# GEGLU feed-forward on one core: program order on every queue but TensorE's, smaller W loads at the half change, and a tail bank by bank

## The chip, the cores and the metric

The kernel runs on one core of a Trainium2 chip. The metric is device time in microseconds for one execution. The core has five engines with a queue each: TensorE (PE in the profile; its weight loads are PEld), VectorE (DVE), ScalarE (ACT), GpSimdE (POOL) and SyncE (SP), which here does nothing but issue DMA transfers. Matmuls write to PSUM, which this kernel divides into 8 banks of 128 x 512 float32.

## What is computed

```python
B, S, D, F = 1, 2048, 1024, 3584      # all bfloat16
def reference(x, w_gate, w_up, w_down):
    return (_gelu(x @ w_gate) * (x @ w_up)) @ w_down     # gelu, tanh form
```

## The kernel before

**Halves.** The 2048 tokens are worked in two halves of 1024 (loop over `h`). For each half the kernel first makes `hT` = gelu(gate) * up, 28 blocks of 128 rows of F by 1024 tokens, and then multiplies it by w_down (`down`). The names `t1`, `bank`, `wd_sb` and so on in the profile are the tiles' names in the code.

**Startup (h = 0 only).** Nine warm matmuls on constants (L164) run while the first data arrives. The first 512 tokens of x come in by plain loads and are transposed on TensorE (L229, evacuated at L209 and L211); the second 512 come in by one transposing DMA (L144). `first_units` then works on three blocks of F at once (NSU = 3, six banks: banks 2 to 7), each with a gate sum and an up sum. For each block ScalarE takes the gelu of the gate sum (`gelu`, L186) and VectorE multiplies it by the up sum (`mult`, L190). After that come five plain units (`unit`, 16 matmuls each at L176, two banks each in rotation): block 3 for the first 512 tokens in banks 0 and 1, then blocks 0 to 3 for the second 512 tokens in banks 2 and 3, 4 and 5, 6 and 7, 0 and 1. A bank can be written again only when its gelu or multiply has read it.

**Pairs.** The remaining blocks are worked two at a time (`pair_quads`) by a Strassen-Winograd scheme: 7 products where the plain form has 8, for gate and for up (j = 0 and 1). It needs four sums and one copy of x blocks (`t1` to `t4`, `b22`, made by `t_sums` at L276 to L280 on VectorE, ScalarE and GpSimdE) once for each half, and four sums and one copy of W blocks (`s1` to `s4` on GpSimdE at L301 to L309, `a22` on ScalarE at L311) for each pair. The sums for the next pair are made during the present one, each in a buffer that TensorE has just read. The half h = 0 has 12 pairs, h = 1 has 14.

**W loads.** w_gate and w_up come in chunks of 512 columns (`new_chunk`, `load_w`), 1 MB each, with two buffers for each matrix; `load_w` for a whole chunk is two transfers of 1 MB.

**Down.** `down` goes over two groups of 512 tokens, each in 14 steps `kk`. A step takes one tile of w_down (`wd_sb`, 512 KB, three buffers) and does 16 matmuls (L423), two in each of the 8 banks; the banks are finished in the last step of the group. ScalarE and VectorE then cast them to bfloat16 (L435, L459), and SyncE stores whole rows. In the very last bank the work is split in two half banks (L444 on VectorE, L451 on ScalarE), each with a store of its own.

**Half change.** During `down` of h = 0 a list `fillers` brings in what h = 1 begins with: each step takes one entry. In the kernel before the entries are one empty, one for all of W chunk 0 (2 MB), 16 transposing loads of x, the sums of W, one for all of W chunk 1 (2 MB), one empty, and the sums of x.

**Order.** A scheduler puts the instructions on each engine's queue. It goes by program order, but may draw one ahead that it takes to be ready earlier. The helper `sp` chains the transfers on SyncE in program order with dependences that order the queue and add no semaphore. `after` does the same for the x sums alone: it puts them behind the last transposition copies, not behind the gelus.

Of the kernel before, what the change touches and what calls it, by code (L numbers as in the profile page):

```python
# [31 lines left out]
def kernel(  # L32
# [67 lines left out]
    last_sp = [None]  # L100

    def sp(inst):

        if last_sp[0] is not None:
            tc.add_manual_dep(
                inst.ins, last_sp[0].ins.name, SCHED_DEP, reason="SP queue order"
            )
        last_sp[0] = inst
        return inst

    def after(inst, other):
        tc.add_manual_dep(inst.ins, other.ins.name, SCHED_DEP, reason="engine order")
        return inst
# [60 lines left out]

    def mm_gu(ps, w_sb, fi, tb, kd):
        return nc.tensor.matmul(  # L176
            ps[:],
            lhsT=w_sb[:, kd, fi * P : (fi + 1) * P],
            rhs=xT[:, kd, tb * TB : (tb + 1) * TB],
            start=(kd == 0),  # L180
            stop=(kd == KD - 1),
        )

    def gelu(ps):
        g_sb = g_pool.tile([P, TB], F32, name="g_sb")
        nc.scalar.activation(out=g_sb[:], in_=ps[:], func=ACT.Gelu_apprx_tanh)  # L186
        return g_sb

    def mult(hT, g_sb, ps, fc, tb):
        nc.vector.tensor_tensor(  # L190
            out=hT[:, fc, tb * TB : (tb + 1) * TB],
            in0=g_sb[:],
            in1=ps[:],
            op=ALU.mult,
        )
# [9 lines left out]
    last_evac = {}  # L205

    def evac(dst, src):
        if evac_ctr[0] % 2 == 0:
            last_evac["dve"] = nc.vector.tensor_copy(out=dst, in_=src)  # L209
        else:  # L210
            last_evac["act"] = nc.scalar.copy(out=dst, in_=src)  # L211
        evac_ctr[0] += 1
# [29 lines left out]
    def first_units(hT):  # L242
        groups = [warm, transpose_x_piece(0)]
        held = [(banks[2 + 2 * u], banks[3 + 2 * u]) for u in range(NSU)]
        bank_ctr[0] = 0
        for kd in range(KD):
            if kd == KPQ - 1:
                bank_ctr[0] = 0
                groups.append(transpose_x_piece(1))
            g = []  # L250
            for j, w_sb in enumerate(chunks[(0, 0)]):
                g += [mm_gu(held[u][j], w_sb, u, 0, kd) for u in range(NSU)]
            groups.append(g)
        for ga, gb in zip(groups[:-1], groups[1:]):
            tc.add_manual_dep(
                gb[0].ins, ga[-1].ins.name, SCHED_DEP, reason="startup PE order"
            )
        for u in range(NSU):
            mult(hT, gelu(held[u][0]), held[u][1], u, 0)
        bank_ctr[0] = 0  # L260


    tsum = {}

    def half(j):
        return slice(j * KH, (j + 1) * KH)

    def t_sums(eng4):
        def b(j, l):
            return xT[:, half(j), l * TB : (l + 1) * TB]  # L270

        for name in ("t1", "t2", "t3", "t4", "b22"):
            tsum[name] = t_pool.tile([P, KH, TB], F32R, name=name)
        sub = ALU.subtract
        tt = nc.vector.tensor_tensor
        first = after(tt(out=tsum["t1"][:], in0=b(0, 1), in1=b(0, 0), op=sub), last_evac["dve"])  # L276
        tt(out=tsum["t2"][:], in0=b(1, 1), in1=tsum["t1"][:].bitcast(F32), op=sub)
        after(nc.scalar.copy(out=tsum["b22"][:], in_=b(1, 1)), last_evac["act"])
        after(tt(out=tsum["t3"][:], in0=b(1, 1), in1=b(0, 1), op=sub), first)
        eng4.tensor_tensor(  # L280
            out=tsum["t4"][:], in0=b(1, 0), in1=tsum["t2"][:].bitcast(F32), op=sub
        )
# [8 lines left out]
    def s_sum(h, pair, j, name):  # L291
# [7 lines left out]
        tt = nc.gpsimd.tensor_tensor  # L299
        if name == "s1":  # L300
            tt(out=t[:], in0=a(1, 0), in1=a(1, 1), op=ALU.add)  # L301
        elif name == "s2":
            s1 = ssum[(h, pair, j, "s1")][:].bitcast(F32)
            tt(out=t[:], in0=s1, in1=a(0, 0), op=ALU.subtract)
        elif name == "s3":
            tt(out=t[:], in0=a(0, 0), in1=a(1, 0), op=ALU.subtract)  # L306
        elif name == "s4":
            s2 = ssum[(h, pair, j, "s2")][:].bitcast(F32)
            tt(out=t[:], in0=a(0, 1), in1=s2, op=ALU.subtract)  # L309
        else:  # L310
            nc.scalar.copy(out=t[:], in_=a(1, 1))  # L311
# [4 lines left out]
    def pair_quads(hT, h, pair, nxt):  # L316
# [20 lines left out]

        b11 = xT[:, half(0), 0:TB]
# [3 lines left out]
        for j in range(2):  # L342
            mm(PB[j], j, block(key, j, 0, 0), b11, True)
            nc.scalar.copy(out=banks[QB[j]][:], in_=banks[PB[j]][:])  # L344
        for j in range(2):
            mm(VB[j], j, s(j, "s1"), tsum["t1"], True)
            m5[j] = m_pool.tile([P, TB], F32, name=f"m5_{j}")
            nc.scalar.copy(out=m5[j][:], in_=banks[VB[j]][:])  # L348
            prep(j, "s1")
        for j in range(2):  # L350
            mm(QB[j], j, s(j, "s2"), tsum["t2"], False)
            nc.scalar.copy(out=banks[RB[j]][:], in_=banks[QB[j]][:])  # L352
            nc.vector.tensor_tensor(  # L353
                out=banks[QB[j]][:], in0=banks[QB[j]][:], in1=m5[j][:], op=ALU.add
            )
# [7 lines left out]
        for j in range(2):  # L363
            mm(RB[j], j, s(j, "s3"), tsum["t3"], False)
            nc.vector.tensor_tensor(  # L365
                out=banks[VB[j]][:], in0=banks[RB[j]][:], in1=m5[j][:], op=ALU.add
            )
# [31 lines left out]
    def down(hT, h, fillers):  # L399
        for grp in range(SH // TB):  # L400
            last_grp = h == NH - 1 and grp == SH // TB - 1
            o_sb = {}
            for kk in range(NKK):
                n = (h * (SH // TB) + grp) * NKK + kk
                while len(wd_tiles) < n + 3:
                    if n + 3 > NH * (SH // TB) * NKK:
                        break
                    if h == 0 and grp == 1 and len(wd_tiles) >= 2 * NKK:
# [4 lines left out]
                wd_sb = wd_tiles[n]  # L413
                for b in range(8):
# [3 lines left out]
                    split = last_grp and kk == NKK - 1 and b == 7  # L418
                    for cc, cw in (
                        [(c0, DN // 2), (c0 + DN // 2, DN // 2)] if split else [(c0, DN)]  # L420
                    ):
                        for c in range(WDT):
                            nc.tensor.matmul(  # L423
                                banks[b][:, cc - c0 : cc - c0 + cw],
                                lhsT=hT[:, kk * WDT + c, ts * P : (ts + 1) * P],
                                rhs=wd_sb[:, c, cc : cc + cw],
                                start=(kk == 0 and c == 0),
                                stop=(kk == NKK - 1 and c == WDT - 1),
                                skip_group_check=True,
                            )  # L430
                    if kk < NKK - 1:
                        continue
                    if dn == 0:
                        o_sb[b // 2] = o_pool.tile([P, D], BF16, name="o_sb")
                        nc.scalar.copy(  # L435
                            out=o_sb[b // 2][:, 0:DN], in_=banks[b][:]
                        )
                        if last_grp and b == 6:
                            sp(nc.sync.dma_start(
                                out=out2[r0 : r0 + P, 0:DN], in_=o_sb[3][:, 0:DN]  # L440
                            ))
                    elif split:
                        hh = DN // 2
                        nc.vector.tensor_copy(  # L444
                            out=o_sb[3][:, DN : DN + hh], in_=banks[b][:, 0:hh]
                        )
                        sp(nc.sync.dma_start(
                            out=out2[r0 : r0 + P, DN : DN + hh],
                            in_=o_sb[3][:, DN : DN + hh],
                        ))  # L450
                        nc.scalar.copy(  # L451
                            out=o_sb[3][:, DN + hh : D], in_=banks[b][:, hh:DN]
                        )
                        nc.scalar.dma_start(
                            out=out2[r0 : r0 + P, DN + hh : D],
                            in_=o_sb[3][:, DN + hh : D],
                        )
                    else:
                        nc.vector.tensor_copy(  # L459
                            out=o_sb[b // 2][:, DN:D], in_=banks[b][:]  # L460
                        )
                        sp(nc.sync.dma_start(
                            out=out2[r0 : r0 + P, :], in_=o_sb[b // 2][:]
                        ))


    for h in range(NH):
        hT = hT_pool.tile([P, KF, SH], BF16, name="hT")
        first_pair = 0
        if h == 0:  # L470
            first_units(hT)
            for fi in range(NSU, FPG):
                unit(hT, (0, 0), fi, 0)
            unit(hT, (0, 0), 0, 1)
            t_sums(nc.gpsimd)
# [3 lines left out]
            for name in S_NAMES:  # L479
                for j in range(2):  # L480
                    s_sum(0, first_pair, j, name)
        for pair in range(first_pair, NPAIR):
# [5 lines left out]
            if pair == NPAIR - 1:  # L488
                for _ in range(2):
# [3 lines left out]
        if h + 1 < NH:  # L493
# [3 lines left out]
            def w_fill(nh=nh):  # L497
                new_chunk((nh, 0))
                load_w((nh, 0), 0, KD, nc.sync)

            def w_fill1(nh=nh):
                new_chunk((nh, 1))
                load_w((nh, 1), 0, KD, nc.sync)
# [6 lines left out]
            fillers = [lambda: None, w_fill]  # L510
# [5 lines left out]
            fillers += [s_fill, w_fill1, lambda: None, lambda: t_sums(nc.gpsimd)]  # L516
# [31 lines left out]
```

## Time and profile before

| what | us |
|---|---|
| device time, median of 3 runs | 567.64 (567.29 to 569.09) |
| span of the profiled execution | 567.4 |
| startup, to the first matmul of the first pair | 40.6 |
| 12 pairs of h = 0 | 151.3 |
| down of h = 0, with the half change | 98.3 |
| 14 pairs of h = 1 | 176.5 |
| down of h = 1 | 96.8 |
| from the last matmul to the end | 3.9 |

The stages are read from TensorE's timeline, from the first matmul of one to the first of the next. TensorE is the engine with the most work, so each stage is best read as TensorE's working time plus the time in which it stands or runs slowly. In the rows of a timeline the bracket at the end gives the idle time of that engine ahead of the instruction and what ended it. An instruction's start is when it runs; the time that it stood in its queue behind others does not show in its own row, only as idle time of its engine with the name of the first one's releaser.

### The profile page before, as it was taken

The numbers are of one execution on the slowest core, as the hardware profiler recorded it, in microseconds if no ns is written. First come the engines' busy times: TensorE is split into PE (matmuls) and PEld (weight loads), VectorE is DVE, ScalarE is ACT, GpSimd is POOL, SyncE is SP. The second block draws the span as 40 slices with busy tenths as digits, with TensorE's granted clock in tenths as the row PEclk, the third lists the DMA queues.
The fourth block names the chain that finished last, engine by engine and source line by source line (L and its number), as shares of the span: only waits on it lengthen the run. The fifth ranks groups of instructions, "written<-read, shape, count | busy, mean of one in ns | idle before, by whom it ended". The sixth has DMA issues, their size and how long they took to land.

```text
span 567.4 us, 6748 instructions
## 1 busy us (share of the span) xinstructions
PE 557.3 (98%) x2523; PEld 335.6 (59%) x2523; DVE 175.2 (31%) x241; ACT 200.8 (35%) x343; POOL 248.3 (44%) x216
## 2 busy tenths in 40 slices
PE   8799999999999999999999999999999999999997
PEld 4347767777677544444457776776777764444443
DVE  0613344444433300123034444334444440001001
ACT  2325555555555200101045555555555540001001
POOL 0456777777666060004037776677777700000000
PEclk9899999999999999999999999999999999999999
DMA  9513404133400197698421331404070003446443
GB/s 274 171 47 102 148 2 148 38 111 113 147 2 0 40 309 198 193 260 281 165 76 27 123 106 43 148 1 148 2 258 3 0 1 118 160 160 231 149 148 111
DMA packets 60960, 67.54 MB, mean 119 GB/s; under 512 B 14592, under 2 KB 44672, under 8 KB 60928
## 3 DMA queue, kind: packets, MB, share of 16 engines
q1 hardware_dynamic: 60240, 66.53, 37.3%
q10 hardware_dynamic: 688, 0.59, 0.3%
q8 instruction: 20, 0.33, 0.2%
q14 instruction: 12, 0.10, 0.1%
HBM read 59.77 MB, written 4.19 MB: 113 GB/s over the span
## 4 chain that ended last, share of the span: by engine, by line
PE 92%; DMA 5%; SPq 1%; ACT 0%; issue 0%; ACTq 0%; DVE 0%; DVEq 0%
PE bank L322 58%; PE bank L423 32%; DMA wu_sb<-in_w_up_dram 3%; PE bank L176 3%; DMA wd_sb<-in_w_down_dram 3%; SPq L144 1%; ACT g_sb L186 0%; SPq L127 0%; ACTq L127 0%; DVE o_sb L444 0%; ACT o_sb L451 0%; DVEq L444 0%; ACT a L311 0%; ACTq L186 0%
## 5 line engine op out<-in xcount | busy, mean ns | idle before, releaser
L423 PE MATMUL bank<-wd_sb,hT 128*128 128x512 bf16 x898 | 194.1, 379 | 1.2 <-DMA wd_sb<-in_w_down_dram 1.2
L322 PE MATMUL bank<-t,s 128*128 128x512 f32 x624 | 161.0, 406 | 0.0
L423 PEld LDWEIGHTS <-hT 128*128 128x128 bf16 x898 | 87.7, 98 | 107.3 <-issue 2.3
L322 PEld LDWEIGHTS bank<-t,s 128*128 128x128 f32 x624 | 117.4, 188 | 29.0
L190 DVE TENSOR_TENSOR hT<-g_sb,bank 128x512 bf16<-128x512 f32 x112 | 76.8, 688 | 73.2 <-ACT g_sb L186 33.5
L186 ACT ACTIVATE g_sb<-bank 128x512 f32<-128x512 f32 x112 | 66.5, 597 | 83.9 <-DVE bank L365 49.9
L301 POOL TENSOR_TENSOR s<-wg_sb 128x512 fp32r<-128x512 bf16 x26 | 31.6, 1217 | 136.6 <-PE bank L322 93.9
L353 DVE TENSOR_TENSOR bank<-bank,m 128x512 f32<-128x512 f32 x52 | 36.4, 700 | 114.0 <-ACT bank L352 114.0
L435 ACT CAST o_sb<-bank 128x512 bf16<-128x512 f32 x16 | 9.4, 586 | 155.7 <-PE bank L423 155.7
L459 DVE CAST o_sb<-bank 128x512 bf16<-128x512 f32 x15 | 10.4, 692 | 164.7 <-PE bank L423 137.9
L322 PE MATMUL bank<-xT,wg_sb 128*128 128x512 bf16 x208 | 53.9, 382 | 0.0
L322 PE MATMUL bank<-xT,wu_sb 128*128 128x512 bf16 x208 | 53.4, 379 | 0.0
L322 PE MATMUL bank<-b,s 128*128 128x512 f32 x208 | 51.4, 389 | 0.0
L322 PE MATMUL bank<-t,a 128*128 128x512 f32 x208 | 51.3, 389 | 0.0
L322 PEld LDWEIGHTS bank<-b,s 128*128 128x128 f32 x208 | 39.0, 188 | 8.2
L322 PEld LDWEIGHTS bank<-t,a 128*128 128x128 f32 x208 | 39.0, 188 | 8.1
L306 POOL TENSOR_TENSOR s<-wg_sb 128x512 fp32r<-128x512 bf16 x26 | 30.3, 1167 | 20.9 <-PE bank L322 20.9
L365 DVE TENSOR_TENSOR bank<-bank,m 128x512 f32<-128x512 f32 x52 | 36.4, 700 | 9.9 <-PE bank L322 9.9
L348 ACT COPY m<-bank 128x512 f32<-128x512 f32 x52 | 30.6, 588 | 17.7 <-PE bank L322 17.7
L352 ACT COPY bank<-bank 128x512 f32<-128x512 f32 x52 | 29.6, 570 | 17.0 <-PE bank L322 17.0
L322 PEld LDWEIGHTS <-wu_sb 128*128 128x128 bf16 x208 | 20.3, 98 | 24.7 <-issue 0.3
L344 ACT COPY bank<-bank 128x512 f32<-128x512 f32 x52 | 29.6, 570 | 14.3 <-PE bank L322 14.3
(33 smaller groups left out, 320.6 us busy)
## 6 DMA issues: line engine op xcount, KB each, us to landing
wd_sb<-in_w_down_dram SPq DMA_DIRECT2D x56, 512.0 KB, 3.6
wg_sb<-in_w_gate_dram SPq DMA_DIRECT2D x13, 1024.0 KB, 5.4
wu_sb<-in_w_up_dram SPq DMA_DIRECT2D x13, 1024.0 KB, 7.5
out_dram<-o_sb SPq DMA_DIRECT2D x15, 256.0 KB, 2.2
xs<-in_x_dram SPq DMA_DIRECT2D x2, 512.0 KB, 5.8
wg_sb<-in_w_gate_dram SPq DMA_DIRECT2D x3, 256.0 KB, 6.8
wu_sb<-in_w_up_dram SPq DMA_DIRECT2D x3, 256.0 KB, 7.0
xT<-in_x_dram SPq DMA_TRANSPOSE x17, 4.2
```

The lines of the kernel that those rows point to most:

```text
L176: return nc.tensor.matmul(ps[:], lhsT=w_sb[:, kd, fi * P : (fi + 1) * P], rhs=xT[:, kd, tb * TB : (tb + 1) * TB], start=(kd == 0), stop=(k ...
L186: nc.scalar.activation(out=g_sb[:], in_=ps[:], func=ACT.Gelu_apprx_tanh)
L190: nc.vector.tensor_tensor(out=hT[:, fc, tb * TB : (tb + 1) * TB], in0=g_sb[:], in1=ps[:], op=ALU.mult,)
L301: tt(out=t[:], in0=a(1, 0), in1=a(1, 1), op=ALU.add)
L306: tt(out=t[:], in0=a(0, 0), in1=a(1, 0), op=ALU.subtract)
L322: nc.tensor.matmul(banks[bank][:], lhsT=lhs[:, c, :], rhs=rhs[:, c, :], start=start and c == 0, stop=c == KH - 1, skip_group_check=True,)
L344: nc.scalar.copy(out=banks[QB[j]][:], in_=banks[PB[j]][:])
L348: nc.scalar.copy(out=m5[j][:], in_=banks[VB[j]][:])
L352: nc.scalar.copy(out=banks[RB[j]][:], in_=banks[QB[j]][:])
L353: nc.vector.tensor_tensor(out=banks[QB[j]][:], in0=banks[QB[j]][:], in1=m5[j][:], op=ALU.add)
L365: nc.vector.tensor_tensor(out=banks[VB[j]][:], in0=banks[RB[j]][:], in1=m5[j][:], op=ALU.add)
L423: nc.tensor.matmul(banks[b][:, cc - c0 : cc - c0 + cw], lhsT=hT[:, kk * WDT + c, ts * P : (ts + 1) * P], rhs=wd_sb[:, c, cc : cc + cw], st ...
```

## The change

It has four parts.

1. **Queues in program order.** A helper `on` chains each instruction on ScalarE, VectorE and GpSimdE to the last one on the same engine, as `sp` did for SyncE. The dependences order the queue and add no semaphore. TensorE's order is left to the scheduler.
2. **The x sums are placed among the first gelus.** `t_sums` becomes `t_sum(name)`, called one sum at a time: t1 ahead of the gelus of the three held blocks, t2 behind their multiplies, b22 and t3 behind unit 3, then the sums of W for the first pair behind unit (0, 1), and t4 behind these.
3. **Smaller W loads at the half change.** Each W chunk comes in four pieces of two transfers of 256 KB, one piece a step. Two pieces of chunk 0 stand between the two sets of 8 transposing loads of x, two behind them; chunk 1 comes last. Three tiles of w_down are asked for ahead of the half's last pairs, where it was two.
4. **Last two steps bank by bank.** In the last group, steps 12 and 13 are merged: for each bank the two matmuls of step 12 and the two of step 13, so that the banks finish one after the other. The last bank is no longer split. In the last group VectorE casts the even banks and ScalarE the odd ones, and the last store is issued from ScalarE.

The core of the diff:

```diff
+    last_on = {}
+    def on(engine, inst):
+        if engine in last_on:
+            tc.add_manual_dep(
+                inst.ins, last_on[engine].ins.name, SCHED_DEP, reason="engine order"
+            )
+        last_on[engine] = inst
+        return inst
...
-    def after(inst, other):
-        tc.add_manual_dep(inst.ins, other.ins.name, SCHED_DEP, reason="engine order")
-        return inst
+    def act(inst):
+        return on("act", inst)
...
+    def t_sum(name):
...
+        if name == "t1":
+            dve(tt(out=t[:], in0=b(0, 1), in1=b(0, 0), op=sub))
...
+        elif name == "t4":
+            t2 = tsum["t2"][:].bitcast(F32)
+            pool(nc.gpsimd.tensor_tensor(out=t[:], in0=b(1, 0), in1=t2, op=sub))
+        else:
+            act(nc.scalar.copy(out=t[:], in_=b(1, 1)))
...
-        nc.scalar.activation(out=g_sb[:], in_=ps[:], func=ACT.Gelu_apprx_tanh)
+        act(nc.scalar.activation(out=g_sb[:], in_=ps[:], func=ACT.Gelu_apprx_tanh))
...
+        t_sum("t1")
         for u in range(NSU):
             mult(hT, gelu(held[u][0]), held[u][1], u, 0)
...
+            steps = [[(kk, b) for b in range(8)] for kk in range(NKK)]
+            if last_grp:
+                steps[-2:] = [[(kk, b) for b in range(8) for kk in (NKK - 2, NKK - 1)]]
...
+                    if dn == (1 if last_grp else 0):
+                        act(nc.scalar.copy(out=dst, in_=banks[b][:]))
+                    else:
+                        dve(nc.vector.tensor_copy(out=dst, in_=banks[b][:]))
+                    if last_grp and b // 2 == 3:
+                        st = (nc.sync if dn == 0 else nc.scalar).dma_start(
+                            out=out2[r0 : r0 + P, c0 : c0 + DN], in_=dst
+                        )
...
             first_units(hT)
+            t_sum("t2")
             for fi in range(NSU, FPG):
                 unit(hT, (0, 0), fi, 0)
+            t_sum("b22")
+            t_sum("t3")
             unit(hT, (0, 0), 0, 1)
-            t_sums(nc.gpsimd)
+            for name in S_NAMES:
+                for j in range(2):
+                    s_sum(0, PPG, j, name)
+            t_sum("t4")
             for fi in range(1, FPG):
                 unit(hT, (0, 0), fi, 1)
...
-            if pair == NPAIR - 1:
-                for _ in range(2):
+            if pair == NPAIR - 2:
+                for _ in range(3):
                     load_wd(len(wd_tiles))
...
+            def w_fill(key, k0):
+                if k0 == 0:
+                    new_chunk(key)
+                load_w(key, k0, k0 + WKP, nc.sync)
...
-            fillers = [lambda: None, w_fill]
+            fillers = [lambda: None]
             for tb in range(NTB):
                 for kd in range(KD):
                     fillers.append(
                         lambda tb=tb, kd=kd: load_xT(xT, nh, tb, kd, kd + 1)
                     )
-            fillers += [s_fill, w_fill1, lambda: None, lambda: t_sums(nc.gpsimd)]
+            fillers = fillers[:9] + w_fills[0][:2] + fillers[9:] + w_fills[0][2:]
+            fillers += [s_fill] + w_fills[1] + [t_fill]
```

More of the change, by code (lines that the diff above doesn't have):

```diff
@@ L98, in next_bank, with dve, pool @@
         return b
-    last_sp = [None]
-    def sp(inst):
[L104 to L108, printed above, removed]
-        return inst
-    def after(inst, other):
-        tc.add_manual_dep(inst.ins, other.ins.name, SCHED_DEP, reason="engine order")
-        return inst
+    last_on = {}
[6 more added lines that the diff above has]
+        return inst
+    def sp(inst):
+        return on("sp", inst)
+    def act(inst):
+        return on("act", inst)
+    def dve(inst):
+        return on("dve", inst)
+    def pool(inst):
+        return on("pool", inst)
     xs0 = xs_pool.tile([P, TSB, D], BF16, name="xs")
@@ L172, with half, b @@
     load_w((0, 1), 0, KD, nc.sync)
+    tsum = {}
+    def half(j):
+        return slice(j * KH, (j + 1) * KH)
+    def t_sum(name):
+        def b(j, l):
+            return xT[:, half(j), l * TB : (l + 1) * TB]
+        t = t_pool.tile([P, KH, TB], F32R, name=name)
+        tsum[name] = t
+        sub = ALU.subtract
+        tt = nc.vector.tensor_tensor
+        if name == "t1":
+            dve(tt(out=t[:], in0=b(0, 1), in1=b(0, 0), op=sub))
+        elif name == "t2":
+            t1 = tsum["t1"][:].bitcast(F32)
+            dve(tt(out=t[:], in0=b(1, 1), in1=t1, op=sub))
+        elif name == "t3":
+            dve(tt(out=t[:], in0=b(1, 1), in1=b(0, 1), op=sub))
+        elif name == "t4":
[3 more added lines that the diff above has]
+            act(nc.scalar.copy(out=t[:], in_=b(1, 1)))
     def mm_gu(ps, w_sb, fi, tb, kd):
@@ L185, in gelu @@
         g_sb = g_pool.tile([P, TB], F32, name="g_sb")
-        nc.scalar.activation(out=g_sb[:], in_=ps[:], func=ACT.Gelu_apprx_tanh)
+        act(nc.scalar.activation(out=g_sb[:], in_=ps[:], func=ACT.Gelu_apprx_tanh))
         return g_sb
     def mult(hT, g_sb, ps, fc, tb):
[L190 to L194, printed above, removed]
+        dve(
+            nc.vector.tensor_tensor(
+                out=hT[:, fc, tb * TB : (tb + 1) * TB],
+                in0=g_sb[:],
+                in1=ps[:],
+                op=ALU.mult,
+            )
         )
@@ L204 @@
     evac_ctr = [0]
-    last_evac = {}
     def evac(dst, src):
         if evac_ctr[0] % 2 == 0:
-            last_evac["dve"] = nc.vector.tensor_copy(out=dst, in_=src)
+            dve(nc.vector.tensor_copy(out=dst, in_=src))
         else:
-            last_evac["act"] = nc.scalar.copy(out=dst, in_=src)
+            act(nc.scalar.copy(out=dst, in_=src))
         evac_ctr[0] += 1
@@ L260, in first_units @@
         bank_ctr[0] = 0
[L263 to L282, printed above, removed]
     ssum = {}
@@ L298, in s_sum, with tt @@
         ssum[(h, pair, j, name)] = t
-        tt = nc.gpsimd.tensor_tensor
+        def tt(in0, in1, op):
+            pool(nc.gpsimd.tensor_tensor(out=t[:], in0=in0, in1=in1, op=op))
         if name == "s1":
-            tt(out=t[:], in0=a(1, 0), in1=a(1, 1), op=ALU.add)
+            tt(a(1, 0), a(1, 1), ALU.add)
         elif name == "s2":
             s1 = ssum[(h, pair, j, "s1")][:].bitcast(F32)
-            tt(out=t[:], in0=s1, in1=a(0, 0), op=ALU.subtract)
+            tt(s1, a(0, 0), ALU.subtract)
         elif name == "s3":
-            tt(out=t[:], in0=a(0, 0), in1=a(1, 0), op=ALU.subtract)
+            tt(a(0, 0), a(1, 0), ALU.subtract)
         elif name == "s4":
             s2 = ssum[(h, pair, j, "s2")][:].bitcast(F32)
-            tt(out=t[:], in0=a(0, 1), in1=s2, op=ALU.subtract)
+            tt(a(0, 1), s2, ALU.subtract)
         else:
-            nc.scalar.copy(out=t[:], in_=a(1, 1))
+            act(nc.scalar.copy(out=t[:], in_=a(1, 1)))
     S_NAMES = ("s1", "s2", "s3", "s4", "a22")
@@ L336, in s, with add_m5 @@
             return ssum[(h, pair, j, name)]
+        def add_m5(dst, src):
+            dve(
+                nc.vector.tensor_tensor(
+                    out=banks[dst][:], in0=banks[src][:], in1=m5[j][:], op=ALU.add
+                )
+            )
         b11 = xT[:, half(0), 0:TB]
@@ L343, in pair_quads @@
             mm(PB[j], j, block(key, j, 0, 0), b11, True)
-            nc.scalar.copy(out=banks[QB[j]][:], in_=banks[PB[j]][:])
+            act(nc.scalar.copy(out=banks[QB[j]][:], in_=banks[PB[j]][:]))
         for j in range(2):
@@ L347, in pair_quads @@
             m5[j] = m_pool.tile([P, TB], F32, name=f"m5_{j}")
-            nc.scalar.copy(out=m5[j][:], in_=banks[VB[j]][:])
+            act(nc.scalar.copy(out=m5[j][:], in_=banks[VB[j]][:]))
             prep(j, "s1")
@@ L351, in pair_quads @@
             mm(QB[j], j, s(j, "s2"), tsum["t2"], False)
[L352 to L355, printed above, removed]
+            act(nc.scalar.copy(out=banks[RB[j]][:], in_=banks[QB[j]][:]))
+            add_m5(QB[j], QB[j])
             prep(j, "s2")
@@ L364, in pair_quads @@
             mm(RB[j], j, s(j, "s3"), tsum["t3"], False)
-            nc.vector.tensor_tensor(
-                out=banks[VB[j]][:], in0=banks[RB[j]][:], in1=m5[j][:], op=ALU.add
-            )
+            add_m5(VB[j], RB[j])
             prep(j, "s3")
@@ L402, in down @@
             o_sb = {}
[L403 to L406, printed above, removed]
+            base = (h * (SH // TB) + grp) * NKK
+            steps = [[(kk, b) for b in range(8)] for kk in range(NKK)]
+            if last_grp:
+                steps[-2:] = [[(kk, b) for b in range(8) for kk in (NKK - 2, NKK - 1)]]
+            for step in steps:
+                kk0 = step[0][0]
+                while len(wd_tiles) < base + kk0 + 3:
+                    if base + kk0 + 3 > NH * (SH // TB) * NKK:
                         break
-                    if h == 0 and grp == 1 and len(wd_tiles) >= 2 * NKK:
+                    if grp == SH // TB - 1 and len(wd_tiles) % (2 * NKK) == 0:
                         break
@@ L412, in down @@
                     fillers.pop(0)()
-                wd_sb = wd_tiles[n]
-                for b in range(8):
+                for kk, b in step:
                     ts, dn = grp * TSB + b // 2, b % 2
@@ L417, in down @@
                     r0 = h * SH + ts * P
[L418 to L430, printed above, removed]
+                    for c in range(WDT):
+                        nc.tensor.matmul(
+                            banks[b][:],
+                            lhsT=hT[:, kk * WDT + c, ts * P : (ts + 1) * P],
+                            rhs=wd_tiles[base + kk][:, c, c0 : c0 + DN],
+                            start=(kk == 0 and c == 0),
+                            stop=(kk == NKK - 1 and c == WDT - 1),
+                            skip_group_check=True,
+                        )
                     if kk < NKK - 1:
@@ L434, in down @@
                         o_sb[b // 2] = o_pool.tile([P, D], BF16, name="o_sb")
-                        nc.scalar.copy(
-                            out=o_sb[b // 2][:, 0:DN], in_=banks[b][:]
-                        )
[L438 to L445, printed above, removed]
-                        )
[L447 to L464, printed above, removed]
+                    dst = o_sb[b // 2][:, c0 : c0 + DN]
+                    if dn == (1 if last_grp else 0):
[5 more added lines that the diff above has]
+                            out=out2[r0 : r0 + P, c0 : c0 + DN], in_=dst
+                        )
+                        if dn == 0:
+                            sp(st)
+                    elif dn == 1:
+                        sp(
+                            nc.sync.dma_start(
+                                out=out2[r0 : r0 + P, :], in_=o_sb[b // 2][:]
+                            )
+                        )
     for h in range(NH):
@@ L478 @@
             first_pair = PPG
-            for name in S_NAMES:
-                for j in range(2):
-                    s_sum(0, first_pair, j, name)
         for pair in range(first_pair, NPAIR):
@@ L495, with t_fill @@
             xT = xT_pool.tile([P, KD, SH], BF16, name="xT")
[L497 to L503, printed above, removed]
+            def w_fill(key, k0):
+                if k0 == 0:
+                    new_chunk(key)
+                load_w(key, k0, k0 + WKP, nc.sync)
+            w_fills = [
+                [lambda k0=k0, c=c: w_fill((nh, c), k0) for k0 in range(0, KD, WKP)]
+                for c in range(2)
+            ]
+            def t_fill():
+                for name in ("t1", "t2", "b22", "t3", "t4"):
+                    t_sum(name)
             def s_fill(nh=nh):
```

## The prediction

> **What bounds the kernel now.** I read the page first: how busy each engine is, then who makes TensorE wait.
>
> ```profile
> span 567.4 us, 6748 instructions
> PE 557.3 (98%) x2523; PEld 335.6 (59%) x2523; DVE 175.2 (31%) x241; ACT 200.8 (35%) x343; POOL 248.3 (44%) x216
> ```
>
> TensorE is busy 98% of the span; no other engine passes 44%. The change alters no matmul's work, so it can only win time in which TensorE stands or runs slowly. The waits of TensorE say where it stands (columns: who waited for whom, total us, times, longest):
>
> ```profile
> PE bank L176 <- ACT g_sb L186: 3.0, 1, 3.0
> PE bank L423 <- DMA wd_sb<-in_w_down_dram: 1.2, 2, 0.7
> ```
>
> One wait for a gelu and two for tiles of w_down. Next the timelines of TensorE and of ScalarE around the first (start, length, engine, line, xcount, idle before):
>
> ```profile
> 18.42 1.89 PE L176 MATMUL bank<-xT,wg_sb 128*128 128x512 bf16 x8
> 20.15 1.89 PE L176 MATMUL bank<-xT,wu_sb 128*128 128x512 bf16 x8
> 25.08 3.41 PE L176 MATMUL bank<-xT,wg_sb 128*128 128x512 bf16 x8 [3.04 <-ACT g_sb L186]
> 28.29 2.09 PE L176 MATMUL bank<-xT,wu_sb 128*128 128x512 bf16 x8
> 30.22 1.89 PE L176 MATMUL bank<-xT,wg_sb 128*128 128x512 bf16 x8
> ```
> ```profile
> 15.89 1.90 ACT L278 CAST b<-xT 128x2048 fp32r<-128x2048 bf16 x1 [2.73 <-DMA xT<-in_x_dram]
> 21.17 0.62 ACT L311 CAST a<-wg_sb 128x512 fp32r<-128x512 bf16 x1 [3.39 <-DMA wg_sb<-in_w_gate_dram]
> 23.91 0.62 ACT L311 CAST a<-wu_sb 128x512 fp32r<-128x512 bf16 x1 [2.12 <-DMA wu_sb<-in_w_up_dram]
> 24.44 2.05 ACT L186 ACTIVATE g_sb<-bank 128x512 f32<-128x512 f32 x4
> ```
>
> ScalarE has two casts of W ahead of the first gelus; they wait for chunk 1 to land (21.17, 23.91), though the sums for those gelus were done near 17.5. Normally eight matmuls take 1.73 us (18.42 to 20.15); after the gap the first eight take 3.21. The windows view gives the clock (the column after the busy times):
>
> ```profile
> 25.10:30.20 5.10, 5.10 (x16) 1.98 (x16) 2.44 (x4) 1.99 (x4) 5.02 (x5) 0.67 0.00 0
> 191.90:290.20 98.30, 97.07 (x450) 43.88 (x450) 12.24 (x11) 7.45 (x11) 15.02 (x9) 1.00 0.71 211
> ```
>
> The second row is the half change, slower than its twin at the end (466.75 to 563.5, without a wait). The chain of waits names its two interruptions:
>
> ```profile
> 199.05 7.58 DMA wd_sb<-in_w_down_dram
> ...
> 262.11 7.32 DMA wd_sb<-in_w_down_dram
> ...
> 563.56 0.44 DVE o_sb L444
> 564.00 0.02 issue
> 564.02 0.37 ACT o_sb L451
> ```
>
> These two tiles land 7.6 and 7.3 us after issue, against a median of 3.6: each lies behind a 2 MB pair of W loads. The last rows are the end: two casts of half a bank, one after the other.
>
> [...] ready gelus stood behind a cast that waited 2.12 us for a transfer. [...] The s1 at 21.22, beside t2 on VectorE, took 2.47 us against 1.17 otherwise. [...]
>
> **The change, part by part.**
>
> *Startup.* Unhindered, the unit (fi 0, tb 1) would begin at 20.15+1.73 = 21.88 and the next at 21.88+3.46 = 25.34. In the trace the next begins at 30.22. The loss is 4.88 us: 3.20 of standing, 1.48 (3.21-1.73) and 0.20 (1.93-1.73) of slow clock. Does the new order free the banks in time? The held sums end at about 17.5 (gate) and 18.15 (up). ScalarE then runs three gelus at 0.51 each (2.05 for four), so bank 2 is free near 18.2. VectorE now has t1 ahead of the multiplies: it waits for xT and runs from 15.99 to 18.28. Behind it are the three multiplies, the first done by 19.0, the last by 20.3 (2.48 for four). TensorE wants bank 2 at 21.88 and bank 3 at 23.61, banks 4 to 7 later still: at least 3.7 us of slack. Next on VectorE are t2 (2.29, to 22.6), the multiply of unit 3 (to 23.3; its banks 0 and 1 are wanted only at 32.3), then t3. On ScalarE b22 follows unit 3's gelu, 20.9 to 22.8; the gelu of unit (0,1) is ready at 23.8; the casts of chunk 1 follow it. So both casts, which wait for transfers, have only later gelus behind them, with over 2 us of slack. I count the full 4.88.
>
> *Sums that move because of it.* GpSimdE now takes s1 of gate, then s1 of up, which waits for the up weights at 23.9, where all four gate sums used to fill that time. Seven sums at 1.16 from 23.9 end at 32.0; a collision with t3 adds up to 1.3 (2.47-1.17), so 33.3. Then t4: 4.10 or 6.01 (both rows exist), by 39.3 at worst. The pairs now start at 40.58-4.88 = 35.70. They want s1 1.7 us in (37.4), s4 9.1 in (44.8) and t4 10.9 in (46.6). All are met: cost nothing.
>
> *Pairs.* In a pair of before ScalarE already has the cast of a22, then the gelu, then the second cast, just as the program is written; VectorE and GpSimdE too. The new dependences order instructions on their own engine. 26 pairs of 12.60 us stay: nothing.
>
> *Half change.* From 191.93 to 290.19 are 98.26 us for 448 matmuls; at 216 ns (3.456 us for each step of 16) that is 96.77. The loss is 1.49. In the new order a step with W carries one w_down tile (512 KB) and two pieces of 256 KB, 1.05 MB in 3.456 us, or 303 GB/s; the trace moved 350 to 390 GB/s during the old bursts. A tile is issued two steps (6.91 us) before its use. It lands in 3.1 to 3.6 alone, and with 512 KB in front, at 360 GB/s, 1.5 later: at most 5.1. Steps with an xT transposition carry no W any more. The second W chunk goes to steps 22 to 25, landed by 285, needed two pairs into the next half. t_sum and s_sum moved to steps 26 and 21 run on engines idle there; xT lands by about 260, the first W chunk by 265, so eight sums and t4 end near 280, before 290. The third tile loaded ahead is no gain: three were already issued together at 137.5. I count 1.49.
>
> *End.* Before: the last matmul ends at 563.47, casts of 0.42 and 0.37 run in series, and the last store is issued at 564.42. After: one cast of 0.59 from 563.56, issue at about 564.18: 0.24 earlier. A store of 128 KB lands in 2.1 us where one of 64 KB took 2.0: net 0.14. Bank by bank needs the last w_down tile after two matmuls of step 12, 0.43 into it: 556.61+0.43 = 557.04. It is issued at 553.13 and lands in 3.5: 556.63. Earlier stores spread out beside matmuls. I count 0.15.
>
> Sum: 567.64-4.88-1.49-0.15 = 561.12, so 561.1.
>
> **The rivals.** *A: the half change keeps a wait.* The W pieces in four steps in a row leave a tile late, or the transposes take more of the DMA engines than I reckon. For it: DMA is 0.9 busy in bursts; against: 1.8 us of slack a tile. Then 1.49 is not won: 562.6. *B: the startup trades one wait for another.* VectorE's t1 waits for xT with three multiplies behind it; a late xT, or a collision with GpSimdE, shifts them. Against: 3.7 us of slack. If TensorE still stands 1.5 us and cools, the gain shrinks by 1.5+1.68: 564.3. *C, slower: strict order adds a wait to every pair.* One cast of 0.62 us exposed in each of 26 pairs costs 16.1: 577.2. For it: each a22 cast waits for TensorE with a gelu behind it. Against: before has this order already, at 0.0 us of TensorE idle in L322. A changed matmul order would fall here too.
>
> **How the numbers follow.** Forecast 0.71, A 0.14, B 0.08, C 0.07. The range reaches from 560.3 (the end gives 0.5 more, and 0.4 of scatter) to 563.4 (A, and 0.8 of scatter), so it holds the forecast and A and leaves out B and C. Faster by over 0.3% means below 565.9: forecast, A, and nearly all of B, 0.91. Same 0.02, from B's tail; slower 0.07, C.
>
> **What would show it.** Right: no wait of L176 on L186; the pairs begin near 35.7; granted clock 1.0 in 21.9 to 30; the two down stages of equal length, 96.8 us, with no wait on wd_sb; pairs still 12.60; one cast after the last matmul. Wrong: a new wait of TensorE on any bank in the pairs, a wait on wd_sb near the transposes or near the end, or a longer pair.

## The result and the profile after

The changed kernel takes 562.95 us (median of 4 runs, 562.21 to 563.71), the kernel before, run beside it, 568.34. The ratio is 0.9907 with a 95% interval of 0.988 to 0.9933: faster, by 5.4 us, inside the forecast range and 1.85 us above the forecast itself. The two traces lie further apart than the medians, by 7.0 us (567.4 and 560.4); why they do is the main question of what follows. One execution of all those below, of `o_order`, took 718.26 us at a granted clock of 0.755, and no figure here includes it.

The head of the page and the waits of TensorE in the changed kernel:

```profile
span 560.4 us, 6719 instructions
PE 552.3 (99%) x2475; PEld 334.9 (60%) x2521; DVE 175.7 (31%) x241; ACT 200.2 (36%) x342; POOL 248.2 (44%) x216
```
```profile
PE bank L265 <- DMA xs<-in_x_dram: 1.2, 1, 1.2
PE bank L172 <- PEq L550: 0.8, 1, 0.8
PE bank L211 <- DMA wu_sb<-in_w_up_dram: 0.2, 1, 0.2
PE bank L211 <- DVE xT L245: 0.2, 1, 0.2
```

The wait for a gelu and the two for w_down tiles are gone, and no new one has come; what is left lies in the first 8 us. (Some matmul records are missing from this trace, so its count is lower.) The timeline of the changed kernel around 20 us:

```profile
17.50 1.58 ACT L221 ACTIVATE g_sb<-bank 128x512 f32<-128x512 f32 x3 [4.38 <-PE bank L211]
18.22 1.88 DVE L226 TENSOR_TENSOR hT<-g_sb,bank 128x512 bf16<-128x512 f32 x3
18.38 1.89 PE L211 MATMUL bank<-xT,wg_sb 128*128 128x512 bf16 x8
20.11 1.89 PE L211 MATMUL bank<-xT,wu_sb 128*128 128x512 bf16 x8
21.84 1.89 PE L211 MATMUL bank<-xT,wg_sb 128*128 128x512 bf16 x7
...
24.26 0.61 ACT L329 CAST a<-wg_sb 128x512 fp32r<-128x512 bf16 x1
...
33.14 4.08 POOL L205 TENSOR_TENSOR t<-xT,t 128x2048 fp32r<-128x2048 bf16 x1
...
35.65 1.03 PE L340 MATMUL bank<-xT,wg_sb 128*128 128x512 bf16 x4
```

The three gelus run as soon as their sums are done, the casts of W come behind, and TensorE goes on at its 1.73 us for eight matmuls. The pairs begin at 35.65, where it was 40.58. The half change is one row of matmuls without a break, up to the first pair of h = 1:

```profile
186.99 96.87 PE L444 MATMUL bank<-wd_sb,hT 128*128 128x512 bf16 x439
283.69 0.81 PE L340 MATMUL bank<-xT,wg_sb 128*128 128x512 bf16 x3
```

That is 96.70 us, where it was 98.26. At the end one cast follows the last matmul, which ends near 556.97 by the chain of waits:

```profile
557.03 0.59 ACT L458 CAST o_sb<-bank 128x512 bf16<-128x512 f32 x1 [1.14 <-PE bank L444]
557.65 0.37 ACTq L462 DMA_DIRECT2D out_dram<-o_sb  x1
```

From the last matmul to the end are 3.4 us instead of 3.9.

### The profile page after: what moved, and what is told of

Its sections match the earlier page's. It is cut to its first block, busy times and chain, and to the rows that moved or that the text cites. A ratio compares the mean times of both kernels' runs of the same rounds, so it can differ in the third digit from the quotient of the medians.

```text
span 560.4 us, 6719 instructions
## 1 busy us (share of the span) xinstructions
PE 552.3 (99%) x2475; PEld 334.9 (60%) x2521; DVE 175.7 (31%) x241; ACT 200.2 (36%) x342; POOL 248.2 (44%) x216
## 4 chain that ended last, share of the span: by engine, by line
PE 98%; DMA 1%; issue 0%; ACT 0%; ACTq 0%
PE bank L340 58%; PE bank L444 34%; PE bank L211 5%; DMA wu_sb<-in_w_up_dram 1%; PE bank L265 0%; ACT o_sb L458 0%; ACTq L135 0%; ACTq L458 0%
## 5 line engine op out<-in xcount | busy, mean ns | idle before, releaser
L316 POOL TENSOR_TENSOR s<-wu_sb 128x512 fp32r<-128x512 bf16 x52 | 62.4, 1200 | 0.1
L340 PE MATMUL bank<-xT,wg_sb 128*128 128x512 bf16 x183 | 52.5, 382 | 1.3
L329 ACT CAST a<-wg_sb 128x512 fp32r<-128x512 bf16 x26 | 16.2, 621 | 54.0 <-PE bank L340 29.2
```

The costliest lines, as they stand in the source:

```text
L316: pool(nc.gpsimd.tensor_tensor(out=t[:], in0=in0, in1=in1, op=op))
L329: act(nc.scalar.copy(out=t[:], in_=a(1, 1)))
L340: nc.tensor.matmul(banks[bank][:], lhsT=lhs[:, c, :], rhs=rhs[:, c, :], start=start and c == 0, stop=c == KH - 1, skip_group_check=True,)
```

## The experiments

**Each part by itself.** `e1_start` has the order and the moved sums, with the half change and the end of before; `e2_half` and `e3_tail` are the kernel before with one part each.

> Parts 1 and 2 alone: program order on the queues and the x sums among the first gelus; half change and end as before. My theory (the gelus stood behind two casts; removing that wins 3.2 us of standing and, where TensorE cools, 1.7 us more): no wait of TensorE for a gelu, pairs begin near 35.7, the stage from there to the end as before with both waits for wd_sb; time 3.2 to 4.9 below before. Rival (the gain of the whole change came mostly from the half change or the end): less than 2 us below before.

```diff
...
-            fillers = [lambda: None]
...
+            fillers = [lambda: None, w_fill]
...
-            fillers = fillers[:9] + w_fills[0][:2] + fillers[9:] + w_fills[0][2:]
-            fillers += [s_fill] + w_fills[1] + [t_fill]
+            fillers += [s_fill, w_fill1, lambda: None, t_fill]
...
```

Measured: 565.9 (565.51 to 566.99), ratio 0.9962 (0.995 to 0.9975), 1.8 us below by the medians. That is less than the 3.2 expected and would fit the rival, so the trace has to decide. In it the wait for a gelu is gone, as TensorE's waits show:

```profile
PE bank L444 <- DMA wd_sb<-in_w_down_dram: 2.7, 2, 2.0
PE bank L265 <- DMA xs<-in_x_dram: 0.9, 1, 0.9
PE bank L172 <- PEq L560: 0.8, 1, 0.8
```

The waits for w_down, 1.2 us before, are 2.7 here: down of h = 0 takes 99.71 us (from 188.35 to 288.06). The pairs begin at 37.01, so against the first trace of before the startup gave 3.57 us, and 1.45 of them were lost at the half change that this kernel kept: the spans differ by 2.2 (567.4 and 565.2).

> Part 3 alone: W in pieces at the half change; startup and end as before. My theory: both waits for wd_sb go, down of h = 0 takes 96.8 instead of 98.3, time 1.5 below before; the wait for the gelu at startup stays at 3.0. Rival (the waits for wd_sb come back in another step): down of h = 0 stays above 97.5 and the time is the same as before.

```diff
...
-            fillers += [s_fill, w_fill1, lambda: None, lambda: t_sums(nc.gpsimd)]
+            fillers = fillers[:9] + w_fills[0][:2] + fillers[9:] + w_fills[0][2:]
+            fillers += [s_fill] + w_fills[1] + [lambda: t_sums(nc.gpsimd)]
```

Measured: 567.01, ratio 0.9976 (0.9965 to 0.9987). There is no wait for `wd_sb`, down of h = 0 is 96.71 (191.38 to 288.09), and the wait for a gelu is still there (2.5). My theory holds for part 3 as a whole. The size of the pieces, their place among the transposing loads and the third w_down tile were changed together, and no run separates them.

> Part 4 alone: last two steps bank by bank, one cast for the last bank. My theory: from the last matmul to the end 3.4 us instead of 3.9 and no wait for the last w_down tile, 0.2 to 0.5 below before. Rival (the last w_down tile comes too late for the merged steps): a wait of TensorE for wd_sb near 557 that eats the 0.5.

```diff
...
+                steps[-2:] = [[(kk, b) for b in range(8) for kk in (NKK - 2, NKK - 1)]]
...
```

Measured: 568.42 (566.87 to 568.87), ratio 0.9997 (0.9986 to 1.0008), which tells nothing by itself: the executions fall into two groups (described below), and 10 of these 14 lie in the upper one, against 15 of the 31 of before beside them. Within the groups it is faster, by 0.4 us: the medians are 567.03 against 567.40 in the lower and 568.53 against 568.98 in the upper. The trace has no wait for the last tile and one cast from 563.61 with the end at 566.9, 3.4 us from the last matmul.

**The queue, turned back.** `e4_two_casts` is the changed kernel with both casts of W ahead of the held gelus, as the scheduler of before had put them.

> The changed kernel with both casts of W chunk 1 for the first pair put ahead of the three held gelus on ScalarE, all else as changed. My theory (head of the queue): the gelus start after the up weights land, near 24.4, TensorE stands 3.0 us for bank 2, then runs at half clock in some executions; 3.2 to 4.9 above the changed kernel and the gain of parts 1 and 2 is gone. Rival (the place of the x sums made the difference, or ScalarE's total work): under 1 us above the changed kernel.

```diff
         t_sum("t1")
+        for j in (0, 1):
+            s_sum(0, PPG, j, "a22")
         for u in range(NSU):
             mult(hT, gelu(held[u][0]), held[u][1], u, 0)
...
```

Measured: 565.44 (565.15 to 566.94), 2.5 above the changed kernel by the medians, which were taken in different sets: less than the 3.2 expected, more than the rival's 1. The timeline of TensorE:

```profile
24.90 3.04 PE L211 MATMUL bank<-xT,wg_sb 128*128 128x512 bf16 x8 [2.83 <-ACT g_sb L221]
27.73 2.47 PE L211 MATMUL bank<-xT,wu_sb 128*128 128x512 bf16 x8
30.03 1.89 PE L211 MATMUL bank<-xT,wg_sb 128*128 128x512 bf16 x8
```

The gap of 2.83 us is back, and behind it sixteen matmuls take 5.13 us instead of 3.46 (rows 2.83 and 2.30 apart, where 1.73 is usual). I call such a slow stretch half clock, since a 128x512 matmul takes 0.43 us in it (nine warm ones in 4.00) and 0.22 otherwise (eight in 1.73). The order of two casts alone brings it back: on ScalarE the second cast runs at 23.73 and the held gelus only at 24.25. The pairs begin at 40.39, 4.74 later than in the trace of the changed kernel, and the spans differ by 4.7 (565.1 and 560.4). The rival is out. Four of the seven executions took 565.15 to 565.44, at a granted clock near 1.00; they probably had the gap without the half clock, but only one of the slower three was traced.

**Two groups of times.** In most of these sets the times fall into two groups. Of 74 executions of the kernel before in the first two sets, 36 lie between 566.89 and 567.71, every one with a mean granted clock of 1.00, and 38 between 568.49 and 569.35, every one at 0.995 to 0.997. The changed kernel's four are 562.2 and 562.3, 563.6 and 563.7. I took it that the clock's coming up early or late at the start made the difference, and varied the warm matmuls: 5 of them, or 11, where the two further ones write to the last bank.

```diff
-    NWARM = 9
+    NWARM = 5
```

> The kernel before with 5 warm matmuls instead of 9. Theory (the executions of a kernel fall into two groups by when TensorE's clock comes up; in the kernel before, a clock that comes up late is hidden, since the gap at 22 ends with the landing of the W chunk and not with TensorE): the clock comes up after 9 us, unit 3 starts 1.3 to 3 us later than 18.4, the wait for the gelu shrinks by as much, no half clock after it; all executions near 567.3, the lower group of before. Rival (the two groups come from transfers or from elsewhere in the program): the later start adds 1.3 to 3 us to both groups.

> The changed kernel with 5 warm matmuls. Theory: here nothing hides a late clock; unit 3 starts 1.3 to 3 us later and the whole time moves with it: 563.6 to 565.3, so the distance to w5_before is only 2 to 3.7. Rival: the distance between the two kernels does not depend on the warm matmuls.

`w5_before`: 567.41, 20 of 22 executions below 567.8, the other two at 569.1. Its trace has the first sixteen transpositions in 1.89 us instead of 1.07, unit 3 at 19.23, 0.8 us later than in the first trace and less than the 1.3 expected, a wait for the gelu of 1.7 and no half clock; the pairs begin at 38.40. `w5_after`: 563.73 (562.92 to 564.32), 3.7 below. Its unit 3 is at 20.19 and its pairs begin at 37.46, both 1.81 later than in the changed kernel. So a late clock is hidden in the kernel before, where the gap ends with the landing of W (pairs at 38.40 here and at 38.60 in `b_again` below, whose clock came up early), and costs its full length, 1.81 us, in the changed one.

> The kernel before with 11 warm matmuls instead of 9, so that TensorE is never idle before the first transposition. Theory: the clock is up early in nearly all executions, the gap is then always near 3 us and followed by half clock; most executions near 569.0, the upper group: more warming makes this kernel slower. Rival (as above): the groups stay as they are, or the time falls.

Measured: 566.67, spread over 563.99 to 568.47: the opposite of what I expected. The timeline of ScalarE shows why:

```profile
20.50 0.62 ACT L311 CAST a<-wg_sb 128x512 fp32r<-128x512 bf16 x1 [2.45 <-DMA wg_sb<-in_w_gate_dram]
21.02 1.57 ACT L186 ACTIVATE g_sb<-bank 128x512 f32<-128x512 f32 x3
23.33 0.62 ACT L311 CAST a<-wu_sb 128x512 fp32r<-128x512 bf16 x1 [0.74 <-DMA wu_sb<-in_w_up_dram]
```

With two more matmuls in front, the scheduler put three gelus between the casts, and TensorE's wait there fell to 0.6. So this run does not test the clock. It shows how loosely the order of before hung together. Its half change was worse, too, in TensorE's timeline:

```profile
267.07 22.57 PE L423 MATMUL bank<-wd_sb,hT 128*128 128x512 bf16 x95 [2.18 <-DMA wd_sb<-in_w_down_dram]
```

A wait of 2.18 us, and then 22.57 us for what takes 20.88 in the other traces. I take these 1.69 us for half clock again: it cost 1.68 after the gap of `before`, and the mean granted clock of this execution is 0.995.

> The changed kernel with 11 warm matmuls. Theory: the clock is up early in nearly all executions, so the upper group (563.6) goes and most executions are near 562.2; the distance to w11_before is 6.5 to 7. Rival: two groups as with 9.

> The changed kernel with 11 warm matmuls once more, to see whether the upper group is really gone. Theory: TensorE has no idle micro-second ahead of the transpositions[...]: all executions between 561.9 and 562.6. Rival (four executions all in the lower group were chance, at even odds one in sixteen): some near 563.6.

Measured: 562.13 (561.98 to 562.47) and 562.29 (562.08 to 562.79), ratios 0.9898 and 0.9897: nine executions, none in the upper group. That is about the time of the changed kernel's lower group. In `e1_start`, which starts as the changed kernel does with 9 warm matmuls, six of eight executions lay in the lower group; at such odds nine of nine would come by chance about once in 13, so it is likely, but not shown beyond doubt, that the two further matmuls removed the upper group. The distance to `w11_before`, 4.5, is not the 6.5 to 7 expected, since that kernel's order had changed.

**A trace of the other group of each kernel.**

> The kernel before once more, for a trace. Theory: if this execution is of the lower group (567.3), the first matmuls are at half clock until about 9 us, unit 3 starts near 19.7, the wait for the gelu is about 1.7 us and no half clock follows it; if of the upper group, it looks like the first trace. Rival: a lower execution with an early clock and a 3 us gap.

> The changed kernel once more, for a trace. Theory: if this execution is of the upper group (563.6), unit 3 starts 1.3 us later than 18.4 and every later stage is shifted by just that; if of the lower group, it looks like the first trace. Rival: the 1.4 us lie in another stage.

`b_again` took 567.41, the lower group. TensorE:

```profile
0.77 3.42 PE L164 MATMUL bank<-const-bfloat16-1.0 128*128 128x512 bf16 x9 [0.77 <-PEq L532]
5.70 1.07 PE L229 MATMUL bank<-ident,xs 128*128 128x128 bf16 x16 [1.50 <-DMA xs<-in_x_dram]
...
24.79 1.89 PE L176 MATMUL bank<-xT,wg_sb 128*128 128x512 bf16 x7 [2.67 <-ACT g_sb L186]
26.52 1.89 PE L176 MATMUL bank<-xT,wu_sb 128*128 128x512 bf16 x8
```

Here my theory falls and its rival is right: the clock came up early, already among the warm matmuls (nine in 3.42 us, against 4.00 in the first trace), the gap is 2.67 us, and no half clock follows it: the rows at 24.79 and 26.52 are 1.73 apart. So the kernel before gets into the lower group by a gap that happens not to be followed by half clock. A late clock is another way in, but only `w5_before`, with 5 warm matmuls, shows it.

`a_again` took 563.26, nearer the upper group (563.6 and 563.7) than the lower, and looks as expected:

```profile
0.77 4.00 PE L172 MATMUL bank<-const-bfloat16-1.0 128*128 128x512 bf16 x9 [0.77 <-PEq L550]
5.79 1.89 PE L265 MATMUL bank<-ident,xs 128*128 128x128 bf16 x16 [1.02 <-DMA xs<-in_x_dram]
7.47 1.49 PE L211 MATMUL bank<-xT,wg_sb 128*128 128x512 bf16 x3
8.78 0.90 PE L211 MATMUL bank<-xT,wu_sb 128*128 128x512 bf16 x3
9.51 0.81 PE L211 MATMUL bank<-xT,wg_sb 128*128 128x512 bf16 x3
```

Sixteen transpositions take 1.89 us instead of 1.07, and the clock is full only near 9 us. The pairs begin at 36.74, 1.09 later than in the first trace, and every later stage is shifted by that. The spans differ by 1.1. The trace of `e1_start` (566.99, the slowest of its eight executions) has the same late clock: its transpositions take 1.89.

**Order without the moved sums.** `o_order` keeps the order but has the x sums and the first W sums where before had them.

> The changed kernel with the x sums all together behind unit (0, 1) and the first pair's W sums behind the units, where the kernel before had them; the queues stay in program order. Theory (part 1, the order, carries the startup gain; part 2, the place of the sums, only has to be early enough): GpSimdE ends its sums near 42.5, s4 is wanted at 44.8; no wait for a gelu, the same two groups as the changed kernel, 562.2 and 563.6. Rival (the sums become the bound of the first pair): TensorE waits for s or t in the first pair, 1 to 5 us more.

```diff
-        t_sum("t1")
...
-            t_sum("t2")
...
+            for name in ("t1", "t2", "b22", "t3", "t4"):
+                t_sum(name)
+            for fi in range(1, FPG):
+                unit(hT, (0, 0), fi, 1)
             for name in S_NAMES:
                 for j in range(2):
                     s_sum(0, PPG, j, name)
...
```

Measured: 563.93 (five executions, 563.69 to 564.83), ratio 0.993 (0.9914 to 0.9947). The rival is right. GpSimdE's timeline:

```profile
31.15 6.00 POOL L205 TENSOR_TENSOR t<-xT,t 128x2048 fp32r<-128x2048 bf16 x1 [29.85 <-DVE t L200]
37.12 1.15 POOL L315 TENSOR_TENSOR s<-wg_sb 128x512 fp32r<-128x512 bf16 x1
```

In strict order the W sums stand behind t4, the first comes at 37.1, and the first pair pays: from the first pair to down are 152.67 us (35.87 to 188.54), where the changed kernel takes 151.34. No wait for a gelu is left. So part 1 removes the gap, and part 2 saves 1.3 us that part 1 would otherwise cost.

## Why the prediction was right, and where its size was off

The 7.0 us between the two first traces are 4.93 at startup, 1.56 at the half change and 0.5 at the end. Between `b_again` and the changed kernel's trace, both of the lower group, the spans differ by 5.2: 2.95, 1.80 and 0.4. The forecast took off 6.52, as 4.88, 1.49 and 0.15.

*Startup, right in mechanism.* Pairs forecast at 35.70, measured at 35.65; GpSimdE's eight W sums forecast to end by 33.3, measured 33.2; t4 by 39.3 at worst, measured 37.2. Against the first trace the stage gained 4.93, forecast 4.88. `e4_two_casts` shows that the queue order of the casts is the cause.

*Startup, wrong in size.* The step that was off is "I count the full 4.88", and with it the sum "567.64-4.88-1.49-0.15". The 4.88 came from a trace of an execution of 569.15 us and holds 1.68 of half clock; it was taken off a median of 567.64 that lay in the group without that half clock. From 569.15 the same sum gives 562.63, and the profiled execution of the changed kernel took 562.21. Against the lower trace, `b_again`, the stage gains 38.60-35.65 = 2.95. And the changed kernel has its own late clock, hidden before: against `a_again` it gains 38.60-36.74 = 1.86. So the term is worth 1.9 to 4.9 us, by when the clock comes up and whether half clock follows the gap. That the result still lay inside the range was luck in part: the room above the forecast was meant for rival A and scatter, A did not come, and the shortfall came from a term that the range did not provide for.

*Pairs, right.* No wait in them; 151.34 us for 12 pairs, 151.35 before.

*Half change, right.* Forecast 1.49, measured 1.56; by itself, in `e2_half`, 1.86 against `e3_tail`, which kept the old loads and ran in the same set (98.57-96.71). What I did not see is that the old form is not constant: against 96.70, its loss is 1.6 to 1.9 in `before`, `b_again`, `e3_tail` and `w5_before`, but 3.0 in `e1_start` and 4.8 in `w11_before`, where 1.7 of it is half clock. In these two the second tile behind W landed after 8.8 us instead of 7.3 to 7.6. Why there is open: both begin the half change earlier, but no run isolates that.

*End, right in direction, small.* Forecast 0.15, measured 0.5: issue after the last matmul fell from 0.95 to 0.68 us, and the remaining 0.2 lies behind the issue, where the last store landed after 1.7 us (128 KB) instead of 2.0 (64 KB); no run shows why.

*Rivals.* A and B did not come: no wait stayed. C neither: strict order added nothing to the pairs. The nearest to it is `o_order`, where order without the moved sums makes TensorE wait for the sums of W in the first pair alone, 1.3 us in all.

## What to carry to other kernels

In `e4_two_casts` two casts that waited for a transfer held three ready gelus on ScalarE until 24.25, where they ran at 17.50 without them, and the pairs began 4.74 us later: place what TensorE waits for ahead of what waits for memory, and fix that order rather than leave it to a scheduler that two more matmuls can turn round, as in `w11_before`. Before you subtract a gain seen in one trace, see which execution the trace shows, and subtract from that one; where times fall into groups, ask what differs in the first 10 us. Look, too, for what a wait for a transfer was hiding before it is removed: here a late clock, worth 1.09 us in `a_again` and 1.81 in `w5_after`, which did not show in nine executions with two more warm matmuls.

## What was not expected of the hardware

Half clock after a gap depends on more than its length: 2.18 us in `w11_before` and 2.54 in `e2_half` were followed by it, 2.67 in `b_again` was not. What decides it, no run here shows.

The cost was the same each time: 1.67 to 1.69 us after the gaps of `before`, `e2_half`, `e3_tail`, `e4_two_casts` and `w11_before`. With 0.43 us for a matmul instead of 0.22 each slow one loses 0.21, so that cost is about eight slow matmuls, an estimated 3.4 us at half clock (8 times 0.43). Where they lie differs, by the same estimate: of the first eight matmuls after the gap about seven were slow in `before` (3.21 us) and about three in `e3_tail` (2.37 us); of the next eight about one (1.93 us) and about five (2.76 us). So in `e3_tail` most of the loss came later behind the gap. What sets the length and the place of the slow stretch was not shown.

In `a_again` 1.02 us without matmuls, between the warm ones and the first transposition, went with a full clock put off to 9 us. The gap alone does not decide this either: `e3_tail` had the same nine warm matmuls in 4.00 us and 1.05 us of idle time, and its transpositions ran at full clock, sixteen in 1.07 us. With 11 warm matmuls, which leave 0.65 us there in the trace of `w11_after`, no execution of the upper group came in nine.

The granted clock does not show the late start. The windows view of `a_again` over the slow transpositions gives 1.00 in the column after the busy times:

```profile
5.60:8.00 2.40, 2.21 (x18) 1.94 (x19) 0.71 (x2) 0.66 (x2) 0.00 (x0) 1.00 1.10 355
```

Over the half clock after the gap of the kernel before it had shown 0.67 (25.10 to 30.20 in `before`). At the start only the spacing of the matmuls tells.
